# A fused attention and adapter kernel: tokens put into natural order at the x copy, other groups, coarser squares

## The chip, the cores and the metric

The kernel runs on one core of one Trainium2 chip. The metric is the device time of one execution in microseconds (us), taken as the median of several runs.

## The reference

Squared-ReLU attention for 8 batches, 12 heads, 448 tokens and head size 64 gives x; a mixture of eight rank-16 adapters, two chosen per token, is added to it.

```python
# q, k, v: (8, 12, 448, 64) float32
scores = scale * np.matmul(q, k.transpose(0, 1, 3, 2))
attn = np.maximum(scores, 0.0) ** 2 / S
x = np.matmul(attn, v)            # then to (3584, 768): token by (head, dim)
logits = x @ w_gate               # (3584, 8)
topk = the two largest logits of each token
w = softmax over these two
delta = sum over the two experts e of w * ((x @ A[e]) @ B[e])   # A[e]: 768x16, B[e]: 16x768
return x + delta                  # (3584, 768) float32
```

## The kernel before

**Loads.** q, k and v come in by DMAs that POOL issues (line 185), converted to bf16. A partition p of 64 takes seven neighbouring tokens, so token p*7+j lies at partition p in block j. Twelve heads are handled as three "quads" q of four heads. For each batch and quad, PE transposes q and k (L310), and DVE copies the transposed tiles to `qT` (L324, L332).

**Attention.** The scores are made in steps n: one step is one block j of 64 keys against all 448 queries of a batch and quad. `qk` (L449) writes scores into two PSUM banks, `relu` (L468 on ACT, L470 on DVE) brings them as bf16 into a tile `a`, `sq` (L485, DVE) squares a whole tile `a` of two or three steps, and `pv` (L516) multiplies with v and accumulates over j. Batch 7 is cut into a part of 320 columns, done block by block, and one of 128, done four blocks at a time (`PARTS`). Columns of qT stand in the order (j, p), so the result and x do too: permuted tokens.

**x.** When the last j is done, `xt_copy` (L544) brings the two PSUM banks of the result into `xt`, the transposed x in bf16 for all 3584 tokens, with one copy of 448 columns for each bank, on ACT or DVE.

**Adapters.** Tokens are taken in 28 tiles of 128. For a group of up to three tiles, `gate` makes x times (A, w_gate) (`z`, L560), the two largest logits (L581), weights by a sigmoid (L585 to L600), weighted z (`zp`, L604), its transpose (`zt`, L622) and the copy `zT` (L639). For each tile and half (384 columns), `b` (L714) multiplies zT with B in float32. Without more, three identity matrix products (L705) add x in PSUM ahead of it, and a copy (L743, ACT or DVE) brings the sum to `osb`. For tiles in a "turned" group, SP issues six DMA transposes (L655) that bring x from `xt` to `xb`; then the identity products fall away and DVE adds xb while it copies (L734). Before the change these are tiles 15 to 23, three at a time.

**Stores.** As tokens are permuted, `st` (L760) writes a tile in two transfers of 64 rows, each row 7 rows from the next in the output. SP issues nearly all; ACT issues those of tiles 24 and 26 and its half of tile 27.

**Order.** The kernel's program order is written out in the string `ORDER`: each word is an operation with the engine (`:A`, `:D`) and the PSUM bank (`@4`). Every engine goes through its own instructions in that order; waits between engines follow from data and buffers. `POOLS` gives the number of buffers of each kind (11 of `a`, 4 of `osb`, 3 of `xb`). `GROUP` is the largest width of `a`.

Of the kernel before, what the change touches and what calls it, by code (L numbers as in the profile page):

```python
# [10 lines left out]
BF16 = mybir.dt.bfloat16  # L11
# [3 lines left out]
J = 7  # L15
CUT = 3
SPIN = 8
PH = 64
QUADS = 3
NB = 8  # L20
# [9 lines left out]
PARTS = {b: ((0, S, 1),) for b in range(NB)}  # L30
PARTS.update({7: ((0, 320, 1), (320, 448, 4))})


C = dict(late=6, xi=(), om=(), merge_x=0, sqs=(2, 2, 3), xback=(15, 23), xblat=1.4, xbdur=1.35, bx=8, xlag=6, xh=2, apart=3, apcap=1, gl=(3, 1), tqlat=2.0)
GROUP = 2688
POOLS = dict(qT=5, a=11, zp=2, zT=3, osb=4, w=3, q=5, k=5, v=8, xb=3)
# [3 lines left out]
f4 f3 f1 f0 f2 f6 f5 f8 f7 f11 f9 f10 f84@0 f12 f88 f85@2 f90 f89 f13 f87@4 qk0@6 f91 qk1@0 qk2@2 relu0:D qk3@4  # L40
f14 relu1:A relu2:D relu3:A tp2@6 f17 qk4@0 relu4:A te2 qk5@4 qk6@2 sq2 relu5:A tp3@6 f16 f86@0 relu6:A te3 sq0
qk7@0 f15 qk8@4 qk9@6 relu7:A tp4@2 relu8:D relu9:A f18 qk10@0 te4 qk11@4 relu10:A qk12@6 sq4 tp5@2 relu11:A f19
qk13@0 relu12:A te5 tp6@4 f26 relu13:A sq9 qk14@2 qk15@6 tp7 relu14:A f23 sq7 pv0@0 pv1 pv2 relu15:A pv3 qk16@2
te6 pv4 pv5 relu16:A f20 pv6 qk17@6 x13:D pv7@4 relu17:A qk18@2 sq11 pv8 f22 pv9 x12:A qk19@6 relu18:A pv10
qk20@0 relu19:D f21 pv11 relu20:A pv12 pv13 qk21@2 x27:A sq16 qk22@6 f27 qk23@0 relu21:A aw1@5 sq14 relu22:A f33
relu23:A x26:D qk24@2 tp8@6 ae1 f25 relu24:A qk25@0 sq18 qk26@4 tp9 relu25:A f55 pv14@2 pv15 pv16 relu26:A pv17
te8 qk27@0 pv18 f31 pv19 relu27:A pv20 sq23 qk28@4 qk29@6 x41:A f28 qk30@0 relu28:A x40:D aw0@3 sq25 relu29:A
f29 relu30:A qk31@4 tp10@6 ae0 tp11 relu31:A f32 sq21 qk32@0 qk33@2 relu32:A te10 pv21@4 pv22 f30 relu33:A pv23
qk34@0 sq30 qk35@6 relu34:A qk36@2 f37 relu35:D relu36:A qk37@0 pv24 pv25 pv26 relu37:A sq32 qk38@2 f35 tp12@6
pv27 relu38:A tp13 qk39@0 x55:A te12 f43 qk40@2 x54:A z0@5 relu39:A sq35 qk41@6 f34 z1 relu40:A qk42@0 relu41:D  # L50
z2 relu42:A qk43@2 f38 gmax0 relu43:A tp14@6 sq28 qk44@0 tp15 relu44:A f42 qk45@2 gd0 gu0 te14 relu45:A qk46@0
gt0 relu46:A f50 sq39 qk47@6 pv28@2 pv29 pv30 gsg0 pv31 relu47:A qk48@0 f24 pv32 pv33 gw0 sq44 pv34 relu48:A f48
qk49@6 x69:A gzp0 tp18@0 relu49:A tp19 sq37 f36 pv35@4 zt0@3 zt1 zt2 x68:A qk50@6 te18 zT0:A pv36 f41 pv37
relu50:A qk51@2 pv38 sq46 pv39 relu51:A pv40 qk52@0 f47 qk53@6 pv41 relu52:A tp16@2 x82:D tp17 relu53:A te16
qk54@0 b2@4 relu54:A sq49 f44 qk55@6 o2:A qk56@2 qk57@0 relu55:A relu56:D b0@4 f49 x83:A relu57:D qk58@6 o0:A
qk59@2 relu58:A z3@5 z4 f39 sq51 relu59:A qk60@0 qk61@6 z5 sq56 relu60:A b4@4 f40 relu61:A gmax3 qk62@2 sq58
b1@0 relu62:A f46 gu3 gd3 o4:A qk63@6 gt3 sq42 qk64@2 gsg3 o1:A b3@1 f65 relu63:A gw3 b5@4 gzp3 relu64:A sq60
f51 zt3@0 zt4 zt5 o3:A pv42@6 pv43 o5:A qk65@2 st2 pv44 zT3:A pv45 sq53 qk66@4 relu65:A pv46 pv47 pv48 tp20@0
relu66:A st4 qk67@2 tp21 x96:D x97:A f53 te20 pv49@4 relu67:A pv50 qk68@6 st0 pv51 pv52 relu68:A pv53 sq63 f66
pv54 pv55 qk69@0 qk70@2 x110:A relu69:D qk71@6 f45 relu70:A b6@4 relu71:A x111:D qk72@0 o6:D tp22@2 relu72:A  # L60
sq65 qk73@6 tp23 pv56@4 pv57 relu73:A f74 qk74@0 te22 pv58 pv59 relu74:A pv60 qk75@6 f79 pv61 sq67 pv62 relu75:A
qk76@2 b8@0 relu76:A x124:D qk77@6 f64 x125:A sq70 tp24@2 relu77:A tp25 qk78@4 z6@1 te24 f59 relu78:A qk79@6 z7
relu79:A o8:D qk80@4 qk81@2 f52 sq72 z8 relu80:A b10@0 relu81:A gmax6 sq77 f54 qk82@6 tp26@4 o10:A tp27 qk83@2
relu82:A gd6 gu6 b7@0 te26 f56 relu83:A qk84@6 gt6 o7:D qk85@4 gsg6 relu84:A qk86@2 gw6 f70 sq74 b9@0 relu85:A
pv63@6 pv64 relu86:A gzp6 pv65 qk87@4 pv66 sq79 pv67 relu87:A pv68 pv69 zt6@1 zt7 x139:A x138:D zt8 qk88@2 o9:A
qk89@4 zT6:D qk90@6 relu88:A st8 relu89:D tp28@0 tp29 relu90:A qk91@2 f80 te28 pv70@4 pv71 relu91:A pv72 pv73
qk92@6 f60 sq84 pv74 pv75 relu92:A pv76 qk93@0 b14@2 x153:D x152:A f58 relu93:A sq81 qk94@6 tp30@4 o14:A tp31
pv77@0 relu94:A pv78 f77 qk95@2 te30 pv79 pv80 relu95:A pv81 qk96@6 pv82 f57 sq91 pv83 relu96:A qk97@4 b11@2
relu97:D x166:A f67 b12@3 x167:A o11:A sq93 qk98@6 o12:A st10 qk99@0 qk100@4 relu98:A relu99:D b13@2 relu100:A
z9@3 st6 sq88 qk101@6 o13:A tp32@0 qk102@4 relu101:A tp33 b15@2 st12 f62 sq86 relu102:A qk103@6 o15:A te32 f61  # L70
qk104@4 relu103:A z10 z11 sq100 relu104:A qk105@0 f69 pv84@6 pv85 pv86 relu105:A gmax9 qk106@4 pv87 sq95 f72
pv88 relu106:A pv89 pv90 qk107@0 x181:A qk108@4 f63 gd9 gu9 x180:A relu107:D b16@2 relu108:A gt9 qk109@6 o16:D
f81 pv91@0 gsg9 pv92 relu109:A gw9 pv93 sq105 qk110@4 pv94 pv95 relu110:A pv96 f78 qk111@6 gzp9 pv97 relu111:A
x195:D zt9@2 zt10 qk112@4 sq98 x194:A zt11 f75 b17@3 relu112:A zT9:D qk113@6 o17:A sq102 pv98@0 qk114@4
relu113:A pv99 st16 tp36@2 pv100 tp37 relu114:A pv101 qk115@6 te36 pv102 pv103 relu115:A st14 pv104 tp34@4 tp35
f83 sq109 qk116@2 x209:A qk117@6 x208:A b20@1 relu116:A f68 te34 b22@0 relu117:A f71 sq114 o20:A qk118@2 qk119@4
qk120@6 relu118:A b21@1 f73 sq112 o22:A b23@2 relu119:A o21:D z12@3 sq107 relu120:A st20 qk121@0 qk122@4
relu121:A z13 relu122:D z14 o23:A qk123@6 pv105@0 gmax12 pv106 relu123:A qk124@4 gd12 pv107 gu12 pv108 gt12
sq116 pv109 relu124:A pv110 pv111 qk125@6 f82 b18@2 gsg12 relu125:A gw12 x223:D x222:A qk126@4 f76 o18:D qk127@6
relu126:A b19@1 gzp12 sq121 relu127:A zt12@0 zt13 zt14 qk128@2 pv112@4 pv113 o19:D relu128:A qk129@6 pv114  # L80
zT12:D pv115 st18 pv116 relu129:A pv117 sq123 pv118 tp38@2 qk130@0 x236:A tp39 qk131@6 st22 relu130:A b24@4 te38
relu131:A tp42@0 sq119 tp43 x237:A qk132@2 b25@6 relu132:A te42 xb90 b28@7 o24:A o25:A sq128 xb93 qk133@2 o28:A
qk134@4 tp40@0 relu133:A sq126 pv119@6 tp41 pv120 relu134:A pv121 xb91 qk135@2 te40 pv122 pv123 relu135:A pv124
pv125 qk136@4 x251:D xb94 qk137@0 x250:A b29@2 sq130 relu136:A b26@3 st24 relu137:A sq135 o29:A qk138@6 qk139@4
o26:A qk140@0 xb92 z15@2 relu138:A relu139:D z16 z17 relu140:A qk141@6 st28 gmax15 pv126@4 pv127 relu141:A gd15
pv128 gu15 qk142@0 gt15 sq133 pv129 pv130 gsg15 pv131 relu142:A xb108 qk143@6 pv132 gw15 b27@3 gzp15 x264:A
x265:D relu143:A zt15@2 xb111 zt16 zt17 sq137 pv133@0 o27:A qk144@4 tp44@6 zT15:A pv134 tp45 relu144:A xb95
qk145@2 pv135 te44 pv136 relu145:A pv137 qk146@4 pv138 pv139 st26 sq140 relu146:A z18@6 b30@7 x279:A sq142 z19
x278:A xb109 qk147@2 qk148@4 qk149@0 o30 relu147:A z20 sq144 b32@7 relu148:A xb112 relu149:A b33@2 gmax18 xb110
qk150@4 o32 qk151@0 relu150:A b31@3 gu18 o33 relu151:A gd18 qk152@4 sq149 st32 b34@7 relu152:A gt18 o31 gsg18  # L90
qk153@0 qk154@4 gw18 o34 relu153:A b35@2 st30 gzp18 relu154:A qk155@0 o35 pv140@6 relu155:A pv141 sq151 qk156@4
xb113 pv142 pv143 relu156:A qk157@2 qk158@0 pv144 pv145 relu157:D relu158:A pv146 tp46@4 tp47 x293:A x292:D
qk159@0 qk160@2 relu159:A zt18@7 te46 zt19 xb126 zt20 z21@6 relu160:A z22 sq156 zT18:A qk161@0 qk162@4 qk163@2
relu161:A xb129 b40@7 sq147 relu162:A z23 sq158 relu163:A qk164@0 xb127 pv147@4 pv148 pv149 relu164:A pv150
qk165@2 o40 pv151 pv152 relu165:A pv153 sq154 qk166@0 xb130 b41@7 relu166:A gmax21 x307:A gu21 qk167@2 gd21
pv154@0 sq163 x306:A pv155 pv156 st34 relu167:A pv157 pv158 qk168@4 gt21 o41 pv159 gsg21 pv160 b36@2 gw21 x320:A
gzp21 xb128 x321:A b38@3 sq161 relu168:A zt21@7 zt22 sq165 zt23 qk169@0 st40 zT21:A pv161@4 pv162 pv163
relu169:A pv164 qk170@6 o38 pv165 pv166 relu170:A o36 pv167 xb131 b37@3 x335:D x334:A sq168 qk171@0 qk172@6
relu171:A qk173@4 z24@2 o37 z25 relu172:A sq170 st36 b46@3 relu173:A b47@0 o46 b39@1 sq172 b44@3 o47 z26 o39
# [831 lines left out]
```

## Time and profile before

| what | value |
|---|---|
| median of 3 runs | 181.65 us (181.2 to 183.14) |
| the profiled execution's own time | 182.88 us |
| its span, first to last instruction | 180.8 us |
| mean granted TensorE clock | 0.988 |
| PE / DVE / ACT / POOL busy | 165.2 / 163.6 / 156.4 / 89.9 us |
| scores on ACT (L468), 158 | 132.6 us, 952 ns each |
| squares on DVE (L485), 75 | 89.0 us, 1200 ns each |
| B products (L714), 112 | 47.5 us, 515 ns each |
| x copies (L544): ACT 37, DVE 17 | 19.0 us and 9.6 us |
| stores issued by SP, 50 of 192 KB | 3.9 us to landing |
| DMA transposes on SP, 18 | 3.1 us to landing |

Busy time is the time in which at least one instruction of an engine runs; instructions in a row overlap, so busy time is less than count times mean. A share of the span says how full an engine is on the average, not which engine sets the pace in a given stretch. In the views, an engine name followed by q is its queue, and PEld is PE's loading of weights. The span is about 2 us shorter than the execution's time.

### The profile page before, as it was taken

Reading aid. Unit: us, or ns where it says so; the run is one execution under the profiler, and the core shown is the slowest. Engines: PE = TensorE matmul, PEld = TensorE weight load, DVE = VectorE, ACT = ScalarE, POOL = GpSimd, SP = SyncE. Lnnn points to the kernel's source line nnn. Section 1 sums busy time; section 2 is a strip of 40 time slices with the busy share of each in tenths; the row PEclk is TensorE's granted clock in tenths of the full one; section 3 lists DMA queues with packets and bytes.
Section 4 is the critical chain, followed back from the end, with each engine's and each line's share of the span. In section 5 each row is a group of like instructions: output and inputs, shape, how many; then the busy total and the mean of one; then the engine's idle time right before and its main releaser. Section 6 shows DMA issues by size and latency. Waiting matters only on the chain.

```text
span 180.8 us, 7744 instructions
## 1 busy us (share of the span) xinstructions
PE 165.2 (91%) x3366; PEld 99.2 (55%) x3366; DVE 163.6 (90%) x254; ACT 156.4 (87%) x240; POOL 89.9 (50%) x155
## 2 busy tenths in 40 slices
PE   7777889788999999999999899999999999999990
PEld 2434466454555565655646475655666557676640
DVE  0799799999989999999999899999999999999740
ACT  3499899999999999999999999999999899992120
POOL 7998998979669377760877487340000000000000
PEclk9997899999999999999999999999999999999999
DMA  5999999999999999996599999997376579467875
GB/s 94 127 175 180 156 142 179 182 184 164 214 142 146 186 237 194 176 178 141 68 143 287 224 181 259 224 170 202 68 126 144 131 175 110 101 149 176 227 215 172
DMA packets 34450, 30.50 MB, mean 169 GB/s; under 512 B 11952, under 2 KB 30896, under 8 KB 34416
## 3 DMA queue, kind: packets, MB, share of 16 engines
q0 software_dynamic: 22000, 17.03, 64.9%
q1 hardware_dynamic: 11792, 11.90, 26.5%
q10 hardware_dynamic: 624, 1.08, 2.2%
q8 instruction: 26, 0.43, 1.0%
q14 instruction: 8, 0.07, 0.1%
HBM read 33.84 MB, written 11.01 MB: 248 GB/s over the span
## 4 chain that ended last, share of the span: by engine, by line
PE 51%; ACT 27%; POOL 7%; DMA 6%; issue 4%; DVE 3%; ACTq 0%; DVEq 0%; POOLq 0%
ACT a L468 24%; PE ps L714 18%; PE ps L449 11%; PE ps L516 10%; DMA q<-in_q_dram 6%; PE ps L560 4%; PE ps L310 3%; PE ps L705 3%; POOL q L185 3%; POOL k L185 3%; PE ps L622 2%; ACT osb L743 2%; DVE a L485 2%; ACT xt L544 1%; POOL k_rest L216 1%
## 5 line engine op out<-in xcount | busy, mean ns | idle before, releaser
L468 ACT ACTIVATE a<-ps 128x896 bf16<-128x896 f32 (+3 forms) x158 | 132.6, 952 | 3.7 <-PE ps L449 3.1
L485 DVE TENSOR_TENSOR a<-a 128x1792 bf16<-128x1792 bf16 (+3 forms) x75 | 89.0, 1200 | 0.0
L449 PE MATMUL ps<-qT 64*64 64x448 bf16 (+2 forms) x756 | 58.1, 342 | 3.9 <-ACT a L468 2.4
L714 PE MATMUL ps<-B,zT 128*128 128x384 f32 x112 | 47.5, 515 | 0.0
L516 PE MATMUL ps<-a,v 64*64 64x448 bf16 (+2 forms) x756 | 45.3, 335 | 1.6 <-DVE a L485 1.3
L449 PEld LDWEIGHTS <-qT 64*64 64x64 bf16 x756 | 25.1, 105 | 31.8 <-issue 23.2
L185 POOL DMA_DIRECT2D k<-in_k_dram x46 | 27.9, 629 | 18.2 <-PE ps L310 7.3
L185 POOL DMA_DIRECT2D v<-in_v_dram x48 | 29.0, 629 | 6.2 <-PE ps L449 1.8
L185 POOL DMA_DIRECT2D q<-in_q_dram x48 | 29.4, 651 | 4.9 <-DMA v<-in_v_dram 2.7
L516 PEld LDWEIGHTS <-v 64*64 64x64 bf16 x756 | 22.7, 108 | 9.0 <-issue 4.1
L324 DVE COPY qT<-ps 128x1792 bf16<-128x1792 bf16 x21 | 22.8, 1085 | 0.2
L544 ACT CAST xt<-ps 128x448 bf16<-128x448 f32 (+2 forms) x37 | 19.0, 554 | 2.9 <-PE ps L516 2.7
L743 ACT COPY osb<-ps 128x384 f32<-128x384 f32 x26 | 13.1, 523 | 7.1 <-PE ps L714 4.1
L714 PEld LDWEIGHTS ps<-B,zT 128*128 128x128 f32 x112 | 17.3, 190 | 3.3 <-issue 0.3
L470 DVE TENSOR_SCALAR a<-ps 128x896 bf16<-128x896 f32 (+1 forms) x16 | 16.9, 1067 | 0.5 <-PE ps L449 0.5
L310 PEld LDWEIGHTS <-q 64*64 64x64 bf16 x672 | 10.4, 111 | 6.3 <-issue 2.5
L560 PEld LDWEIGHTS <-xt 128*128 128x128 bf16 x168 | 10.5, 98 | 5.8 <-issue 4.7
L560 PE MATMUL ps<-awg,xt 128*128 128x136 bf16 x168 | 13.5, 223 | 0.0
L705 PEld LDWEIGHTS <-xt 128*128 128x128 bf16 x114 | 8.0, 98 | 9.9 <-issue 8.1
L310 PE MATMUL ps<-identb,q 64*64 64x64 bf16 x672 | 10.8, 196 | 2.5 <-DMA q<-in_q_dram 1.3
L705 PE MATMUL ps<-identb,xt 128*128 128x128 bf16 x114 | 12.7, 220 | 0.2
L544 DVE CAST xt<-ps 128x448 bf16<-128x448 f32 (+2 forms) x17 | 9.6, 571 | 2.2 <-PE ps L516 2.2
(47 smaller groups left out, 97.5 us busy)
## 6 DMA issues: line engine op xcount, KB each, us to landing
out_dram<-osb SPq DMA_DIRECT2D x50, 192.0 KB, 3.9
q<-in_q_dram POOLq DMA_DIRECT2D x48, 112.0 KB, 4.8
v<-in_v_dram POOLq DMA_DIRECT2D x48, 112.0 KB, 5.0
k<-in_k_dram POOLq DMA_DIRECT2D x46, 112.0 KB, 5.1
out_dram<-osb ACTq DMA_DIRECT2D x4, 192.0 KB, 2.9
B<-in_moe_B_dram POOLq DMA_DIRECT2D x1, 384.0 KB, 8.0
xb<-xt SPq DMA_TRANSPOSE x18, 3.1
a_raw<-in_moe_A_dram POOLq DMA_DIRECT2D x1, 192.0 KB, 5.2
```

The costliest lines, as they stand in the source:

```text
L185: nc.gpsimd.dma_start(out=t[g * PH : g * PH + PH], in_=k.qkv[w][b, g, :, 2 * q : 2 * q + 2, :])
L310: nc.tensor.transpose(k.ps_b[sl * PH : sl * PH + PH, o.banks[g], (w * J + j) * PH : (w * J + j) * PH + PH], source(w, j)[r, sl], k.identb[ ...
L324: nc.vector.tensor_copy(t.rearrange("p g w x -> p g (w x)"), k.ps_b[:, m.banks[0] : m.banks[0] + 2, : 2 * S])
L449: nc.tensor.matmul(out=bank(o, sl)[g * PH : g * PH + PH, at : at + w], lhsT=t[r, g, 1, j * PH : j * PH + PH], rhs=t[r, g, 0, x0:x1], start ...
L468: nc.scalar.activation(out, flat(qk_ops[n], w), ACTF.Relu, scale=k.relu_scale)
L470: nc.vector.tensor_scalar(out, flat(qk_ops[n], w), k.relu_scale, 0.0, op0=ALU.mult, op1=ALU.max)
L485: nc.vector.tensor_mul(a, a, a)
L516: nc.tensor.matmul(out=bank(head, g)[sl * PH : sl * PH + PH, :w], lhsT=vn[r, sl, j * PH : j * PH + PH], rhs=T["a", g0][r, x + sl * width(n ...
L544: evac(w, lambda cp, g=g: cp(k.xt[:, g * QUADS + q, b * S + x0 : b * S + x1], bank(src, g)[:, :w]), deps=[pv_ops[n]], free=[(src, g)], key ...
L560: nc.tensor.matmul(out=bank(zops[0])[:, t * ZW : t * ZW + ZW], lhsT=k.xt[:, do, 128 * tiles[t] : 128 * tiles[t] + 128], rhs=k.awg[:, do, : ...
L705: nc.tensor.matmul(out=out(h)[:, x * 128 : x * 128 + 128], lhsT=k.xt[:, 3 * h + x, c0 : c0 + 128], rhs=k.identb, start=(x == 0), stop=Fals ...
L714: nc.tensor.matmul(out=o, lhsT=T["zT", g0][:, zi], rhs=rhs, start=xb is not None, stop=True, skip_group_check=True,)
```

## The change

x is brought into natural token order while it is copied from PSUM: the copy reads its source with a step of 64 words and writes without gaps. For batches 0 to 5 one copy takes both banks. Gate groups are cut so that they end with batches (3, 3, 3, 3, 2, 3, 2, 2, 3, 3, 1 tiles). Turned are tiles 17 to 20 in one group of four, 21 to 23 and 24 to 26; 15 and 16 no longer. Stores are single transfers of 128 neighbouring rows. Squares take four and three steps in turn between step 14 and step 140; `a` has 8 larger buffers for 11. Batch 7's parts are 322 and 126 tokens. The string `ORDER` is another one throughout; it is left out here.

```diff
-PARTS.update({7: ((0, 320, 1), (320, 448, 4))})
-C = dict(late=6, xi=(), om=(), merge_x=0, sqs=(2, 2, 3), xback=(15, 23), xblat=1.4, xbdur=1.35, bx=8, xlag=6, xh=2, apart=3, apcap=1, gl=(3, 1), tqlat=2.0)
-GROUP = 2688
-POOLS = dict(qT=5, a=11, zp=2, zT=3, osb=4, w=3, q=5, k=5, v=8, xb=3)
+PARTS.update({7: ((0, 322, 1, (0, 1, 2)), (322, 448, 4, (0, 1, 2)))})
+C = dict(late=6, xi=(), om=(), merge_x=126, sqp=((14, (2, 2, 3)), (140, (4, 3)), (999, (2, 2, 3))), om2=(), fl=(), gf=(3, 3, 3, 3, 2, 3, 2, 2, 3, 3, 1), ai=4, tg=((17, 4), (21, 3), (24, 3)), sp=(), xbdur=1.45, bx=8, xh=2, apart=3, apcap=1, gl=(3, 1), tqlat=2.0)
+GROUP = 3584
+POOLS = dict(qT=5, a=8, zp=2, zT=3, osb=4, w=3, q=5, k=5, v=8, xb=2)
...
 # qk
-                            out=bank(o, sl)[g * PH : g * PH + PH, at : at + w],
-                            lhsT=t[r, g, 1, j * PH : j * PH + PH], rhs=t[r, g, 0, x0:x1],
+                            out=bank(o, sl)[g * PH : g * PH + PH, at : at + w].rearrange("k (j p) -> k j p", j=J),
+                            lhsT=t[r, g, 1, j * PH : j * PH + PH],
+                            rhs=t[r, g, 0].rearrange("d (j p) -> d j p", j=J)[:, :, x0 // J : x1 // J],
...
 # xt_copy
-                evac(2 * w, lambda cp: cp(k.xt[:, q::QUADS, b * S + x0 : b * S + x1], pair(src)[:, :, :w]),
+                evac(2 * w, lambda cp: cp(k.xt[:, q::QUADS, b * S + x0 : b * S + x1].rearrange("d g (p j) -> d g p j", j=J),
+                                       pair(src)[:, :, :w].rearrange("d g (j p) -> d g p j", j=J)),
...
-            evac(w, lambda cp, g=g: cp(k.xt[:, g * QUADS + q, b * S + x0 : b * S + x1], bank(src, g)[:, :w]),
+            evac(w, lambda cp, g=g: cp(k.xt[:, g * QUADS + q, b * S + x0 : b * S + x1].rearrange("d (p j) -> d p j", j=J),
+                                       bank(src, g)[:, :w].rearrange("d (j p) -> d p j", j=J)),
...
 # st
-            r = 0
-            while r < 128:
-                b, x = divmod(c0 + r, S)
-                j, p = divmod(x, PH)
-                m = min(PH - p, 128 - r)
-                if b >= c["bx"]:
-                    j = TURNED[j]
-                {"SP": nc.sync, "ACT": nc.scalar, "POOL": nc.gpsimd}[e].dma_start(
-                    out=k.out[b, j, p : p + m, c1:c2], in_=T["osb", tl][r : r + m, c1:c2])
-                r += m
+            {"SP": nc.sync, "ACT": nc.scalar}[e].dma_start(out=k.out[c0 : c0 + 128, c1:c2], in_=T["osb", tl][:, c1:c2])
...
-    h.out = out.rearrange("(b p j) f -> b j p f", b=NB, j=J)
+    h.out = out
```

## The prediction

> **What bounds the kernel now.** I read the page's busy times first, then busy time by stretch of the span, then the chain of the last stretch, then single instructions.
>
> ```profile
> PE 165.2 (91%) x3366; PEld 99.2 (55%) x3366; DVE 163.6 (90%) x254; ACT 156.4 (87%) x240; POOL 89.9 (50%) x155
> ```
>
> No engine stands out on the average, so the stretches decide. Columns: stretch, its length, busy time of PE, PEld, DVE, ACT, POOL, granted clock, DMA share, GB/s.
>
> ```profile
> 6.00:30.00 24.00, 19.55 (x488) 11.52 (x489) 21.92 (x25) 21.38 (x28) 22.99 (x39) 0.93 1.18 162
> 30.00:60.00 30.00, 26.85 (x607) 15.94 (x603) 29.36 (x42) 30.00 (x46) 24.96 (x43) 1.00 1.13 173
> 60.00:90.00 30.00, 29.40 (x701) 17.93 (x700) 29.90 (x41) 30.00 (x44) 16.64 (x29) 1.00 0.98 169
> 120.00:150.00 30.00, 29.90 (x643) 18.52 (x640) 29.35 (x48) 28.80 (x48) 0.00 (x0) 1.00 0.66 144
> 165.00:171.00 6.00, 6.00 (x105) 4.12 (x95) 5.16 (x22) 1.56 (x7) 0.00 (x0) 1.00 0.79 212
> 171.00:181.00 10.00, 4.89 (x28) 2.65 (x26) 2.79 (x5) 1.13 (x3) 0.00 (x0) 0.95 0.67 191
> ```
>
> Three regimes. Up to 30 us POOL's loads are the bound: POOL 22.99 of 24, PE only 19.55. From 30 to 150 us ACT and DVE are both full and PE nearly so: less work helps there only if it comes off ACT or DVE. From about 161 us (the last score product ends at 160.88) PE alone is the bound. The chain of the last stretch says it exactly (start, length, what):
>
> ```profile
> 173.28 0.17 PE ps L705 x3
> 173.45 0.70 PE ps L714 x2
> 174.15 0.17 PE ps L705 x3
> 174.32 0.70 PE ps L714 x2
> 175.02 0.17 PE ps L705 x3
> 175.19 0.71 PE ps L714 x2
> 175.90 0.02 issue
> 175.92 0.56 DVE osb L743
> ```
>
> Each output half of tiles 24 to 27 costs 0.17 us for three identity products that add x and 0.70 us for z times B. After the last copy come stores; the timeline has ACT's queue issuing them from 174.70 for 2.94 us, so to 177.64, and the span ends 3.2 us later at 180.8.
>
> **What consecutive instructions really cost.** Mean durations overlap their neighbours, so I take distances between starts in the timeline (start, length, what):
>
> ```profile
> 69.41 1.08 DVE L324 COPY qT<-ps 128x1792 bf16<-128x1792 bf16 x1
> 70.41 1.55 DVE L485 TENSOR_TENSOR a<-a 128x2688 bf16<-128x2688 bf16 x1
> 71.88 0.62 DVE L544 CAST xt<-ps 128x448 bf16<-128x448 f32 x1
> 72.41 1.08 DVE L485 TENSOR_TENSOR a<-a 128x1792 bf16<-128x1792 bf16 x1
> 73.41 1.08 DVE L324 COPY qT<-ps 128x1792 bf16<-128x1792 bf16 x1
> ```
>
> A square of 1792 takes 1.00 us, of 2688 1.47 us: 0.47 us per 896, hence 0.06 us fixed and 1.94 us for 3584 (estimate from these two). An x copy of 448 takes 0.53 on DVE. On ACT seven scores in a row take 5.89 us, 0.82 each, and a 448 copy 0.42 (start 64.10, next start 64.52).
>
> **The change, part by part**, with instruction counts from the two orders of instructions.
>
> *Coarser squares.* 75 squares become 57 over the same elements: 18 x 0.06 = -1.1 us of DVE.
>
> *x copied whole.* 24 copies of 448 on ACT become 12 of 2x448, on DVE 12 become 6: 12 x (2 x 0.42 - 0.82) = -0.2 us on ACT, 6 x (2 x 0.53 - 1.00) = -0.4 on DVE. This uses the contiguous price for reads that now step 64 words through PSUM at every element; see the second rival. By the Trainium skill ("ScalarE: Activation LUTs", What ACT_TABLE_LOAD costs) an instruction with immediates has 186 ns fixed, of which 93 ns overlap, so 12 merged pairs would save 12 x 93 ns, about 1.1 us; the starts above show 0.02 us each, so I do not take it.
>
> *Other moves between ACT and DVE.* Outputs: ACT copies 26 to 22, at 0.365 us (two in 0.73), -1.5; DVE adds 18 to 20 and copies 12 to 14, +1.9 at 0.47. zT: DVE -0.9, ACT +0.8. One more gate group (11 for 10): DVE +0.6, ACT +0.2. The remaining score and x shapes come to +0.3 on ACT, -0.2 on DVE. Summed: ACT -0.4, DVE -0.1. So in the full stretch the change is worth almost nothing: I take -0.2.
>
> *Tiles 15 and 16 by PE, 24 to 26 by transposes.* After the last score product the order now has 14 output halves in place of 15 (-0.70) and 2 identity triples in place of 8 (6 x 0.17 = -1.02): -1.72 us on the engine that sets the end. Cover: the six transposes of tiles 24-26 come on SP's queue between stores, about 1.25 us each and 3.1 us to landing; the last two wait for the last large x copies, but the first add needing them stands behind the whole gate of tiles 24-26 and several B products, over 5 us of PE work. Without that cover it would be up to +2. DVE makes all their adds, at 0.5 us against PE's 0.70 per half, and still keeps up. Before the last score product PE gets one half and four triples more, +1.4 us; PE has 4.7 us idle between 30 and 165 us, mostly early, so I take +0.4 (0 to +1.4).
>
> *Plain stores.* One issue of 128 rows for two of 64. Between tiles nothing waits for SP. At the end ACT and SP each issue one transfer for two: an issue takes 1.18/2 = 0.59 us, so -0.59 (bounds -0.6 to +0.3, if one larger transfer lands later by half a landing spread). The stores of tiles 4 and 9 now stand far back in SP's order and each holds one of the four output buffers for long; the next users of the remaining buffers come 7 or more scores (over 5 us) after the store before them, above the 3.9 us of a landing. Cost 0, up to +1.
>
> *Start.* v of the first triple is loaded two loads earlier (about 2.4 us), so value products can fill PE's holes (4.45 us idle from 6 to 30 us); but the two selector operations (0.84 and 0.83 us) move ahead of the next batch's k on POOL. PE's waits for loads are short:
>
> ```profile
> PE ps L310 <- DMA q<-in_q_dram: 1.3, 3, 0.6
> PE ps L516 <- DVE a L485: 1.3, 2, 0.7
> ```
>
> I take -0.5 (-1.5 to +1.5).
>
> *Sum.* -0.2 - 1.72 + 0.4 - 0.59 - 0.5 = -2.6 us. The profiled execution took 182.88 us (span 180.8 and 2.1 around it), so 180.3 there. It lay 1.23 us above the median of the runs, 181.65; against the median the forecast is 179.0 us. With the bounds the case spans 176.5 to 180.5.
>
> **Rivals.**
>
> *1. The tail gain is given back.* PE is full from 120 us on (29.90 of 30), so the +1.4 us moved ahead of the last score product may count whole, and the denser end (1.40 us per tile for 1.74, with 393 KB each, so 280 GB/s where the last stretches show 191 to 212) may wait for output buffers, about +0.7. Then -2.6 + 1.0 + 0.7 = -0.9: 180.8 us. Against: 0.67 DMA share at 191 GB/s leaves room to about 285.
>
> *2. The stepped PSUM read is slow: slower than before.* Every x copy now writes natural order, reading words 256 bytes apart. No row of this trace steps so. The nearest rows that show one engine at two rates by form are DVE's: 1792 bf16 in 1.00 us against 896 f32 from PSUM in 1.00, a factor of two, which I use as the upper bound; the lower is no penalty. ACT reads 14,850 such elements per partition (12 x 896, 4 x 448, 6 x 322, 3 x 126) at 0.91 ns: doubled +13.5 us, some 12 of it in the full stretch, where nothing hides it because the engine of each instruction is fixed. DVE would get +7.4 beside it. Time 191 at a factor of two, 182 at a quarter more; it decides from about a fifth more per copy (2.6 of 12). Centre 187. I take no penalty because these copies handle one f32 word per step, already the slow form. The Trainium skill speaks against me ("Advanced Engine Details and Errata", PSUM Cachelines): PSUM lines hold two f32 values, and accesses should come in contiguous pairs for best throughput, said of matmuls. No run here shows it yet.
>
> *3. Coarse squares block DVE.* A square of 3584 holds DVE 1.94 us; a score or transposed-q copy behind it waits, and PE behind that. The waits row shows up to 0.7 us for one. At 0.3 us for 18 squares, +5.4, less the gain: 184.5. For: DVE has no idle time. Against: value products stand seven scores behind the scores that they need, which covers one square.
>
> **How the numbers follow.** Forecast 0.58, rival 1 0.15, rival 2 0.17, rival 3 0.10. A measurement of this kernel tells about 1% from no change: faster is below 179.8, slower above 183.5. Forecast gives 0.52 faster, 0.06 same; rival 1 0.02, 0.10 and 0.03 slower; rival 2 0.02 same, 0.15 slower; rival 3 0.10 slower. Sums: 0.54, 0.18, 0.28. The range 176.0 to 186.0 leaves out the strong half of rival 2 and a gain beyond every bound; the forecast's own range is 176.5 to 180.5.
>
> **What would show it.** Right: ACT's 2x448 copies at about 0.99 us mean like the 896 scores; the last score product near 160 us; 13.3 us of PE from there to the last product, with 0.70 us steps for tiles 24 to 26; one store issue per queue after the last copy. Wrong: 2x448 copies above 1.2 us (rival 2); PE waiting for DVE's squares by several us (rival 3); the last product as late as 175 us, or output copies waiting for stores (rival 1).

## The result, and the profile after

The changed kernel takes 187.16 us (median of 5 runs), the one before 182.57 us (5 runs): a ratio of 1.0258, 95% interval 1.0211 to 1.0306. The change costs 2.6%. The forecast was 179.0 us. The ratios here and below are not quotients of the medians: they leave out executions more than 1.5% above the fastest of their kernel, which are two of these five, two of e1's four, five of twelve in e10 and in e15, and up to three of twelve elsewhere. The profiled execution took 189.69 us, of which some 2.8 us go with a low clock at its end, as will be seen; it is read for waits and order, and totals come from the ratios.

In each of the following views the line numbers are those of the kernel shown: L451 is `qk`, L471 `relu`, L488 `sq`, L519 `pv`, L559 the whole x copy, L643 `zt`, L676 the transpose, L727 the identity product, L736 `b`, L763 the add of a turned tile, L772 the plain output copy, L782 the store.

The page, busy times. No engine has become much fuller; what grew is the span, by 7 us to 187.9.

```profile
PE 168.2 (90%) x3360; PEld 100.5 (54%) x3360; DVE 163.4 (87%) x238; ACT 155.6 (83%) x227; POOL 90.3 (48%) x155
```

Busy time by stretch (stretch, its length, PE, PEld, DVE, ACT, POOL, granted clock, DMA share, GB/s):

```profile
120.00:150.00 30.00, 30.00 (x605) 18.83 (x598) 29.12 (x47) 28.95 (x48) 1.19 (x2) 1.00 0.50 119
...
165.00:171.00 6.00, 6.00 (x121) 4.46 (x120) 5.15 (x17) 2.04 (x6) 0.00 (x0) 1.00 0.26 52
171.00:181.00 10.00, 6.04 (x17) 2.92 (x15) 4.86 (x15) 0.21 (x1) 0.00 (x0) 0.75 0.81 294
181.00:188.00 7.00, 2.63 (x8) 1.22 (x7) 0.93 (x2) 0.48 (x1) 0.00 (x0) 0.74 0.31 115
```

Up to 171 us PE is as full as before. From 171 us PE has holes and a clock of 0.75. Just before, from 165 to 171 us, the DMAs move only 52 GB/s at a share of 0.26: whatever comes late there does not wait for bandwidth.

The page's groups name waits of the output operations (line, engine, operation, tiles, count | busy, mean ns | idle before, and what ended it). No output operation waited for a store before.

```profile
L772 ACT COPY osb<-ps 128x384 f32<-128x384 f32 x22 | 11.0, 505 | 9.4 <-DMA out_dram<-osb 9.1
...
L763 DVE TENSOR_TENSOR osb<-ps,xb 128x384 f32<-128x384 f32 x20 | 10.5, 551 | 6.0 <-DMA out_dram<-osb 3.9
```

The chain of the last stretch (start, length, what) shows where those stores had been:

```profile
163.30 1.01 ACT a L471
164.31 0.65 ACT xt L564 x2
...
166.10 1.21 SPq L676
...
167.36 2.68 SPq L676
...
170.10 2.57 DMA out_dram<-osb
...
172.69 1.02 DVE osb L763 x2
...
174.12 2.52 DMA out_dram<-osb
...
176.73 0.56 DVE osb L763
...
177.74 0.48 PE ps L643
178.22 2.57 PE ps L736 x4
```

Two stores end waits in this chain, and the first could not be issued before 170.10 because SP was busy with transposes (SPq L676). SP's queue in order of time says why:

```profile
153.81 2.71 SPq L782 DMA_DIRECT2D out_dram<-osb  x3
162.44 7.60 SPq L676 DMA_TRANSPOSE xb<-xt  x4
170.10 1.05 SPq L782 DMA_DIRECT2D out_dram<-osb  x2
171.24 2.78 SPq L676 DMA_TRANSPOSE xb<-xt  x2
```

SP does nothing from 156.5 to 162.4 us. Its own waits name what it waits for, in the stretch from 150 us (who, for whom: us, times, longest):

```profile
SPq L676 <- DVE osb L763: 5.9, 1, 5.9
```

The next instruction in SP's queue is the first transpose of tiles 24 to 26, and it waits for a DVE add. The transposes write `xb`. The change has three turned groups and cuts `POOLS` from `xb=3` to `xb=2`, so the third group takes the buffer of the first (tiles 17 to 20), and that is free only when the last add of tile 19 has read it. DVE makes these last adds here:

```profile
160.89 1.49 DVE L763 TENSOR_TENSOR osb<-ps,xb 128x384 f32<-128x384 f32 x3
...
172.69 1.02 DVE L763 TENSOR_TENSOR osb<-ps,xb 128x384 f32<-128x384 f32 x2 [2.44 <-DMA out_dram<-osb]
...
176.73 0.56 DVE L763 TENSOR_TENSOR osb<-ps,xb 128x384 f32<-128x384 f32 x1 [1.51 <-DMA out_dram<-osb]
```

The first three end at 162.38, and SP goes on at 162.44. Behind its four transposes (7.60 us) stand the stores of tiles 18 and 19, whose data were complete by 162.4 and which go out at 170.10. Until then they hold two of the four output buffers; the adds of tile 21 and then of tile 25 wait for one (2.44 and 1.51 us), and with them PE:

```profile
PE ps L736 <- DVE osb L763: 2.4, 1, 2.4
```

At the end the clock adds to the damage. PE is mostly idle from 172 to 178 us, and then four B products take 2.57 us, 0.64 each. The first line is PE's longest pause, in brackets; the others are stretches as above, with the granted clock third from the end:

```profile
175.27 0.91 PE L736 MATMUL ps<-B,zT 128*128 128x384 f32 x2 [2.40 <-DVE osb L763]
...
176.00:178.00 2.00, 0.44 (x2) 0.26 (x2) 1.24 (x4) 0.00 (x0) 0.00 (x0) 0.52 1.02 402
178.00:180.00 2.00, 2.00 (x5) 1.09 (x5) 1.28 (x4) 0.00 (x0) 0.00 (x0) 0.50 0.53 209
180.00:182.00 2.00, 2.00 (x7) 1.00 (x6) 0.65 (x2) 0.00 (x0) 0.00 (x0) 0.50 0.52 203
```

In the profile of e2, below, the same products take 0.32 us. The Trainium skill ("TensorE: Matmul & The Clock Gate", Part 1: The HAM clock gate) says that PE falls to half clock after an idle window of some 3.4 us. The granted 0.50 agrees with the half. The length is not what these runs show: PE worked 2.05 us in the 6 us from 172 to 178, and its longest pause before the clock fell was 2.40 us. In e1, below, a pause of 2.26 us was followed by 0.50 as well; in e15 one of 1.42 us left the clock at 1.00.

### The profile page after: what moved, and what is told of

Read it like the earlier page. It is cut to its first block, busy times and chain, and to the rows that moved or that the text cites. A ratio compares the mean times of both kernels' runs of the same rounds, so it can differ in the third digit from the quotient of the medians.

```text
span 187.9 us, 7650 instructions
## 1 busy us (share of the span) xinstructions
PE 168.2 (90%) x3360; PEld 100.5 (54%) x3360; DVE 163.4 (87%) x238; ACT 155.6 (83%) x227; POOL 90.3 (48%) x155
## 4 chain that ended last, share of the span: by engine, by line
PE 42%; ACT 24%; DMA 12%; DVE 7%; issue 5%; POOL 5%; SPq 2%; ACTq 0%; DVEq 0%; POOLq 0%
ACT a L471 20%; PE ps L736 11%; PE ps L451 11%; PE ps L519 9%; DMA k<-in_k_dram 5%; DMA out_dram<-osb 4%; PE ps L312 4%; DMA q<-in_q_dram 3%; PE ps L581 3%; PE ps L727 2%; POOL q L184 2%; SPq L676 2%; ACT xt L559 2%; DVE a L488 2%; PE ps L643 1%
## 5 line engine op out<-in xcount | busy, mean ns | idle before, releaser
L471 ACT ACTIVATE a<-ps 128x896 bf16<-128x896 f32 (+2 forms) x158 | 131.9, 942 | 6.5 <-PE ps L451 5.7
L488 DVE TENSOR_TENSOR a<-a 128x2688 bf16<-128x2688 bf16 (+5 forms) x57 | 85.9, 1524 | 0.0
L451 PE MATMUL ps<-qT 64*64 64x448 bf16 (+2 forms) x756 | 60.0, 346 | 4.7 <-ACT a L471 2.0
L736 PE MATMUL ps<-B,zT 128*128 128x384 f32 x112 | 48.9, 533 | 2.4 <-DVE osb L763 2.4
L519 PE MATMUL ps<-a,v 64*64 64x448 bf16 (+2 forms) x756 | 45.0, 334 | 0.2 <-ACT a L471 0.2
L451 PEld LDWEIGHTS <-qT 64*64 64x64 bf16 x756 | 24.9, 106 | 33.5 <-issue 26.5
L519 PEld LDWEIGHTS <-v 64*64 64x64 bf16 x756 | 23.1, 107 | 8.8 <-issue 2.5
L736 PEld LDWEIGHTS ps<-B,zT 128*128 128x128 f32 x112 | 18.6, 201 | 6.7 <-DVE osb L763 3.3
L772 ACT COPY osb<-ps 128x384 f32<-128x384 f32 x22 | 11.0, 505 | 9.4 <-DMA out_dram<-osb 9.1
L473 DVE TENSOR_SCALAR a<-ps 128x896 bf16<-128x896 f32 (+2 forms) x16 | 16.9, 1060 | 1.5 <-PE ps L451 1.0
L763 DVE TENSOR_TENSOR osb<-ps,xb 128x384 f32<-128x384 f32 x20 | 10.5, 551 | 6.0 <-DMA out_dram<-osb 3.9
L581 PE MATMUL ps<-awg,xt 128*128 128x136 bf16 x168 | 13.3, 223 | 0.4 <-ACT xt L559 0.4
L727 PE MATMUL ps<-identb,xt 128*128 128x128 bf16 x108 | 12.5, 226 | 0.7 <-ACT xt L559 0.4
L312 PE MATMUL ps<-identb,k 64*64 64x64 bf16 x644 | 10.6, 196 | 1.8 <-DMA k<-in_k_dram 1.8
L727 PEld LDWEIGHTS <-xt 128*128 128x128 bf16 x108 | 7.5, 101 | 8.5 <-issue 7.8
L312 PE MATMUL ps<-identb,q 64*64 64x64 bf16 x672 | 10.3, 195 | 1.7 <-DMA q<-in_q_dram 1.5
```

Source lines behind the costliest of these rows:

```text
L312: nc.tensor.transpose(k.ps_b[sl * PH : sl * PH + PH, o.banks[g], (w * J + j) * PH : (w * J + j) * PH + PH], source(w, j)[r, sl], k.identb[ ...
L451: nc.tensor.matmul(out=bank(o, sl)[g * PH : g * PH + PH, at : at + w].rearrange("k (j p) -> k j p", j=J), lhsT=t[r, g, 1, j * PH : j * PH ...
L471: nc.scalar.activation(out, flat(qk_ops[n], w), ACTF.Relu, scale=k.relu_scale)
L473: nc.vector.tensor_scalar(out, flat(qk_ops[n], w), k.relu_scale, 0.0, op0=ALU.mult, op1=ALU.max)
L488: nc.vector.tensor_mul(a, a, a)
L519: nc.tensor.matmul(out=bank(head, g)[sl * PH : sl * PH + PH, :w], lhsT=vn[r, sl, j * PH : j * PH + PH], rhs=T["a", g0][r, x + sl * width(n ...
```

## The experiments

The theory (the queue theory, Q in the expectations): the whole loss is this one wait of SP, a shortage of `xb` buffers that holds transposes, behind them stores, behind them output buffers. Against it stood that the transposes are late by themselves, that the loss lies in the attention phase (theory M; more PE work there, the coarse squares, or the stepped or whole x copies), and that three turned groups are simply too many. Ratios are against the kernel before, run on the same chip beside it, with their 95% interval; single executions of one kernel lie up to 4% apart, so 1 us needs the ratios. Line numbers shift by a few from kernel to kernel. "Last scores" is the end of the last `qk` in a kernel's profile: 160.88 us before, 163.23 after, with the last product at 175.90 and 183.6.

**e1: the four transposes behind the two stores.** A change of `ORDER` alone.

```diff
-... xb144 ... xb147 ... xb145 ... xb148 ... st36 ... st38 x334:A ...
+... st36 ... st38 xb144 xb147 xb145 xb148 x334:A ...
```

> The changed kernel, only with the first four transposes of tiles 24-26 placed behind the stores of tiles 18 and 19 on SP. Theory Q (SP's queue: the transposes wait for the transpose buffer and the x copies while finished tiles stand behind them unsent, so output buffers run out at the end): these two stores go out near 163 us of the span and not at 170, the adds' wait of 2.4 us goes, and the time falls by 2 to 4 us, to about 184. Theory M (the loss lies in the attention phase, more work on TensorE and later loads, and the end only shows it): same time within 1 us.

Measured: 1.0154 [1.0057, 1.0252], from two executions. By its middle less than half of the loss is gone; with both intervals, a gain is not certain. The profile shows the order: SP's queue now sends the two stores (L780) in time, and the transposes (L674) are what comes late; the chain's wait has changed its name:

```profile
152.66 8.92 SPq L780 DMA_DIRECT2D out_dram<-osb  x5
161.67 9.34 SPq L674 DMA_TRANSPOSE xb<-xt  x6
171.11 8.75 SPq L780 DMA_DIRECT2D out_dram<-osb  x5
```

```profile
167.18 3.63 DMA xb<-xt
...
171.11 2.52 DMA out_dram<-osb
```

With two `xb` buffers, whichever of the two goes first on one queue, the other is late. The half clock comes again, after a pause of 2.26 us:

```profile
174.73 0.35 PE L641 MATMUL ps<-identf,zp 128*128 128x128 f32 x1 [2.26 <-DVE zp L623]
...
176.00:178.00 2.00, 2.00 (x7) 1.06 (x6) 0.89 (x2) 0.00 (x0) 0.00 (x0) 0.50 0.99 387
```

**e2: a third xb buffer.**

```diff
-..., v=8, xb=2)
+..., v=8, xb=3)
```

> The changed kernel with three transpose buffers for two, so that the transposes of tiles 24-26 need not wait until the adds of tiles 17-20 have freed one. Theory Q: they leave SP some 3 us sooner, the stores of tiles 18 and 19 too, time down 1.5 to 3 us. Theory M: no change.

Measured: 182.06 us, 0.9989 [0.9924, 1.0055]: the loss is gone, with order, groups, squares and copies of the changed kernel untouched. SP's queue:

```profile
156.12 5.21 SPq L676 DMA_TRANSPOSE xb<-xt  x4
161.43 2.60 SPq L782 DMA_DIRECT2D out_dram<-osb  x2
164.12 2.52 SPq L676 DMA_TRANSPOSE xb<-xt  x2
166.72 8.94 SPq L782 DMA_DIRECT2D out_dram<-osb  x5
```

The four transposes begin 6.3 us earlier (156.12 for 162.44) and the two stores 8.7 us earlier. No add or copy waits for a store any more, and the chain ends as a chain of PE:

```profile
172.55 1.29 PE ps L736 x4
173.84 0.17 PE ps L727 x3
174.01 0.70 PE ps L736 x2
174.71 0.17 PE ps L727 x3
174.88 0.71 PE ps L736 x2
175.59 0.02 issue
175.61 0.48 ACT osb L772
```

The two profiles can be set against each other from the last scores on. From 162.44 to the `zt` of the last tile (172.44) e2 needs 10.0 us, the changed kernel 14.5 (163.23 to 177.74): 4.5 us more, of which PE's two pauses are 2.40 and 1.56. From there to the last copy e2 needs 3.2, the changed kernel 5.9: 2.8 us of half clock.

**e15: six output buffers instead, xb left at two.**

```diff
-..., osb=4, w=3, ..., xb=2)
+..., osb=6, w=3, ..., xb=2)
```

> The changed kernel as it is (two transpose buffers) with six output buffers for four. Theory Q has two parts: late transposes and, behind them, stores that hold the output buffers. With two more buffers no add or copy waits for a store; the waits for the transposes themselves stay. So the time falls by 2 to 3.5 us from 187, to 184 or 185, and not to e2's 182. If the waits for output buffers are the whole loss: 182; if only the transposes' lateness counts: no change.

Measured: 1.0148 [1.0110, 1.0185], so 1.1 of the 2.6% are gone. SP's idle time is still there, 5.9 us long, and the transposes run from 160.20 only; no add waits for a store, but one waits 1.9 us for its transpose:

```profile
DVE osb L763 <- DMA xb<-xt: 1.9, 1, 1.9
...
PE ps L736 <- DVE osb L763: 1.4, 1, 1.4
```

On one base of 181.7 us the stages are: changed 186.4, stores first 184.5, six output buffers 184.4, three xb buffers 181.5. Each is uncertain by 0.7 to 1.8 us. Of 4.9 us, 2.0 (uncertain by 1.1) are output buffers held by stores that stand behind transposes, and 2.9 (uncertain by 1.4) are left where no add waits for a store. In e15's profile the late transposes make the way from the last scores to the last product 15.00 us (161.29 to 176.29) for e2's 13.15, at a clock of 1.00; what makes the rest of the 2.9 was not shown.

**e3: tiles 24 to 26 not turned.** Their adds go back to identity products, as before the change.

```diff
-tg=((17, 4), (21, 3), (24, 3))     ORDER: xb144 to xb149; o48 to o53 as DVE adds
+tg=((17, 4), (21, 3))              ORDER: none of these;  o48:D o49:A o50:A o51:D o52:D o53:A
```

> The changed kernel with tiles 24-26 not transposed by DMA: identity products add x again (18 more, 1.0 us of TensorE after the last scores), and their output copies are shared between ACT and DVE. Theory Q: SP only stores at the end, no add or copy waits for a store, and in spite of the 1.0 us the time falls by 3 to 4.5 us, to 183 or 184. Theory M: it rises by 1 us.

Measured: 1.0100 [1.0030, 1.0170], between e2 and the changed kernel. Without a third group two buffers are enough and no stall is there, but PE has its six triples back: last scores at 162.91, last product at 177.35, so 14.4 us against 13.15 in e2. The third group, given a buffer of its own, is worth 1.3 us by the two profiles and 2.0 by the two ratios, whose intervals are some 1.2 us to either side.

**e6: the coarse squares cut in two.** On top of e2, each square of 3584 as two instructions of 1792.

```diff
-            nc.vector.tensor_mul(a, a, a)
+            h = 1792 if total == 3584 else total
+            for y in range(0, total, h):
+                nc.vector.tensor_mul(a[:, y : y + h], a[:, y : y + h], a[:, y : y + h])
```

> The changed kernel with three transpose buffers (e2), every square of 3584 made by two instructions of 1792 in the same place. If the coarse square saves what two starts in a row say, 18 x 0.06 us, DVE has 1.1 us more to do and the last scores end up to 1 us later than in e2; if coarse squares block what stands behind them, earlier by 1 us or more. No change beyond 0.5 us: their size does not matter.

Measured: 1.0035 [1.0001, 1.0069], against 0.9989 for e2, with last scores at 162.48 against 162.44. There is no sign that coarse squares block anything, and 18 instructions fewer bring no time that could be told.

**e10: PE work taken out of the middle.** e2 without the identity products of tiles 11 to 16, 12 triples or 2.04 us of PE.

```diff
-                for x in range(0 if xb or xi else 3):
+                for x in range(0 if xb or xi or 11 <= tl <= 16 else 3):
...
-                    start=xb is not None, stop=True, skip_group_check=True,
+                    start=xb is not None or 11 <= tl <= 16, stop=True, skip_group_check=True,
```

> The changed kernel with three transpose buffers (e2), with the identity products of tiles 11 to 16 left out, so that their outputs lack x: 12 triples of 0.17 us, 2.0 us of TensorE, between about 110 and 150 us. If TensorE sets the pace there: last scores 2.0 us earlier than in e2 and time 2.0 us less, near 180. If ACT and DVE set it: no more than 0.5 us earlier; then the products moved ahead of the last scores are not what makes the changed order's last scores late.

Measured: 0.9939 [0.9899, 0.9980], last scores at 161.70. For 2.04 us less PE work that is 0.74 us at the last scores and 0.9 by the ratios. But the changed kernel, e2 and e15, with all of that work in the same order, have theirs at 163.23, 162.44 and 161.29, further apart than 0.74 although only numbers of buffers differ. Whether PE sets the pace before the last scores, as its 30.00 of 30 us from 120 to 150 suggests, stays open.

**e4: natural order and plain stores alone.** The new code with the order, groups, turned tiles, squares and x copies of before.

```diff
-merge_x=126, sqp=((14, (2, 2, 3)), (140, (4, 3)), ...), gf=(3, 3, 3, 3, 2, ...), tg=((17, 4), (21, 3), (24, 3)); GROUP = 3584; a=8, xb=2
+merge_x=0, sqp=((999, (2, 2, 3)),), gf=(), tg=((15, 3), (18, 3), (21, 3)); GROUP = 2688; a=11, xb=3; ORDER of before
```

> The kernel before with only the natural order of tokens: stepped x copies of one bank each, one store of 128 rows per tile, parts of 322 and 126; order, groups, turned tiles 15-23 and squares as before. Theory Q and theory M alike: the stepped copies cost nothing, the end has one store issue less per queue, so 0.5 to 1 us faster than the kernel before, 181 to 182. A theory that the natural order itself costs (stepped reads, larger stores landing later): 185 or more.

Measured: 1.0015 [0.9937, 1.0093], no change. From the last copy to the end of the span it takes 3.9 us, for 4.3 before and 4.3 in e2. Over all the profiles here this stretch is 2.9 to 4.9 us long, so what one store for two saves at the end cannot be told.

**e8: e4 with tiles 15 to 17 not turned.**

```diff
-tg=((15, 3), (18, 3), (21, 3))     ORDER: xb90 to xb95; o30 to o35 as DVE adds
+tg=((18, 3), (21, 3))              ORDER: none of these; o30:D to o35:D as copies
```

> The natural order alone (e4), and tiles 15-17 not turned: 18 identity products more on TensorE before the last scores (6 triples of 0.17 us, 1.0 us), output copies on DVE as before, six transposes less on SP. If TensorE sets the pace from 120 us on: last scores 1.0 us later than in e4 and the time 1.0 us longer. If TensorE's idle time covers it: no change.

Measured: 0.9995 [0.9958, 1.0032]. Six triples more, 1.02 us of PE, are not to be seen; but the difference from e4 is uncertain by 1.6 us, so that they are free there is not shown.

**e5, e12, e14: the third turned group in the old order.** e5 is e4 with tiles 24 to 26 turned and a buffer of their own (`xb=4`); e12 turns 24 and 25 only; e14 is e5 with six output buffers.

```diff
-tg=((15, 3), (18, 3), (21, 3)), xb=3, osb=4
+e5:  tg=(..., (24, 3)), xb=4;  ORDER: xb144 xb147 after xb131, xb145 xb148 after x334, xb146 after st36, xb149 after st46, o48 to o53 on DVE
+e12: as e5, but tg=(..., (24, 2)), o52:A o53:A
+e14: as e5, with osb=6
```

> The natural order alone (e4), and tiles 24-26 turned besides 15-23, with four transpose buffers; their six transposes stand where their x copies are long done, none ahead of a finished tile's store by more than two. Theory Q says that turning the last tiles pays once SP isn't blocked: six identity triples less after the last scores, 6 x 0.17 us, so 1.0 us faster than e4: last product about 14 us after the last scores instead of 15, about 180.5 us. Rival: SP's stores come late again and the end is as long as in e4 or longer.

> e5 with tiles 24 and 25 turned, not 26, whose output copies go to ACT: two triples more on TensorE at the end (0.34 us), two adds less on DVE (1.0 us). In e5 the end ran through DVE: TensorE waited 0.5 us for the last gate behind the adds. If that wait is worth more than the triples: 0.2 to 0.5 us faster than e5; if TensorE alone sets the end: 0.3 us slower.

> e5 (order of before, natural tokens, tiles 24-26 turned too) with six output buffers for four. If output buffers held by stores that leave late still cost at the end of e5, up to 0.7 us faster than e5, about 180.3 us; if not, the same.

Measured: e5 0.9966 [0.9931, 1.0000], e12 0.9950 [0.9919, 0.9980], e14 0.9939 [0.9908, 0.9970], with a median of 180.78 us the lowest found: about 0.6% under the kernel before. The three do not stand apart by their intervals, and e4's overlaps them. The profiles tell more: from the last scores to the last product e4 needs 15.03 us, e5 14.50, e14 14.33 and e12 15.08. In e12's profile a store wait of the familiar kind is still in the chain:

```profile
166.24 3.80 DMA out_dram<-osb
```

and in those of e5 and e14 none is, though their chains run through DVE's adds there. So turning the last tiles shortens the end in the old order by 0.5 to 0.7 us, half to two thirds of the 1.02 us of the six triples; the 0.9 us between the ratios of e4 and e5 are uncertain by 1.6.

**e7, e9, e11, e13: the form of the x copies.** e7 and e9 are e4 with whole x copies, every third on DVE; e7 puts each at the place of the later of the two halves, e9 at that of the earlier. In e7 the next product then overwrites one bank before it is copied, so a part of its x is not the reference's, and e9 replaces it. e11 is e5 with the copies of e9. e13 goes the other way: e2 with each whole copy cut in two halves side by side, one on ACT and one on DVE.

```diff
-e4:  ... x27:A ... x26:D ...   merge_x=0
+e7:  ... x26:A ...             merge_x=126   (in the place of x26:D)
+e9, e11: ... x26:A ...         merge_x=126   (in the place of x27:A)
-e2:  ... x12:A ...             merge_x=126
+e13: ... x12:A x13:D ...       merge_x=0
```

> The natural order alone (e4), and the two banks of x of batches 0 to 5 copied by one instruction, in the place of the later of the two. By starts in a row 0.2 us of ACT and 0.4 us of DVE less: same time as e4 within 0.5 us, a copy of 2x448 at 0.95 us on ACT and 1.09 on DVE. Rival: the two banks come free later and the next value products wait, 1 us slower or more.

> The natural order alone (e4), and the two banks of x of batches 0 to 5 copied by one instruction in the place of the earlier of the two, where both banks are finished. By starts in a row 0.2 us of ACT and 0.4 us of DVE less: e4's time within 0.5 us. Rival: a copy of 2x448 holds its engine for twice as long and scores behind it come late, 1 us slower or more.

> The order of before with natural tokens, tiles 24-26 turned too (e5), and x copied whole as in e9. If whole copies save what starts in a row say, 0 to 0.5 us faster than e5: about 180.6 us, 0.5 per cent under the kernel before.

> The changed kernel with three transpose buffers (e2), x of batches 0 to 5 again copied by two instructions, one on ACT and one on DVE in the same place, 448 columns each. In the order of before whole copies cost 5 us and more (e9); if they cost here too, the last scores end 2 us or more earlier than in e2 and the time falls to 180 or less. If this order was laid out around whole copies: same as e2 within 0.7 us, or slower, as each engine is interrupted twice as often.

Measured: e7 1.0475 [1.0430, 1.0521], e9 1.0317 [1.0281, 1.0354], e11 1.0261 [1.0217, 1.0305], e13 1.0436 [1.0381, 1.0490]. All four lose 5 to 9 us. If whole copies were dear, e13 was to gain, and it lost. The copies themselves (L556) cost in e9 what they cost elsewhere:

```profile
L556 ACT CAST xt<-ps 128x896 bf16<-128x896 f32 x12 | 11.3, 944 | 0.5 <-PE ps L516 0.5
```

What is lost is lost between engines. From 30 to 150 us PE, DVE and ACT of e4 are busy for 115.25, 117.88 and 118.40 of 120 us; those of e9 for 110.74, 112.03 and 113.15, 4.5 to 5.9 us less. In e13 they are at 110.21, 110.97 and 111.60, and its waits show the scores on PE (L449) behind copies of qT and x on DVE (L324, L562):

```profile
PE ps L449 <- DVE qT L324: 3.0, 5, 1.3
...
PE ps L449 <- DVE xt L562: 2.3, 4, 1.0
```

e13 also puts 12 more x copies on DVE, 18 halves for 6 whole ones, and that is a part of its loss; its size was not separated. What follows is narrower than hoped: an order written by hand fits the lengths that it was written for, and a change of form inside it cost more here than the form. So the middle parts of this change (order, groups, copies) cannot be priced one by one in this way.

## Why the prediction was wrong, point by point

**The step that failed is the cover of the transposes of tiles 24 to 26**, "come on SP's queue between stores", with "between tiles nothing waits for SP" beside it. It asked when their data are there and who needs them, and not where they are written. The diff has `xb=2`, the change has three turned groups, and each group but the first two must wait for an older one's last reader: SP stood 5.9 us before the first of them. The bound "up to +2" without cover, for which the prediction gives no working, was too small. The cure by one buffer is worth 4.9 us (e2): 2.0 of it, uncertain by 1.1, through stores that stand behind the transposes (e15), which the prediction had at "cost 0, up to +1" and for another reason, the early stores of tiles 4 and 9. And an idle PE then fell to half clock, which cost 2.8 us in the profiled execution and was in no step. The transposes took 1.9 us each here (7.60 for four) and 1.3 in e2 (5.21), where 1.25 had been used.

**The range did not follow from the bounds.** The terms' own bounds, without the +2 for a lost cover, add up to -4.0 and +2.3 us on 181.65, so 177.6 to 183.9, where 176.5 to 180.5 was given. The 187.16 lies outside both.

**Rival 1** had the mark right, output copies that wait for stores, and the cause wrong: it spoke of 280 GB/s, and the wait arose at 52. Its 0.7 us for it came from bandwidth.

**The tail's PE work was right.** From the last scores to the last product 13.3 us were forecast; e2, without the stall, has 162.44 to 175.59, 13.15.

**What was to come before it was not.** The last scores were to come some 0.3 us earlier than the 160.88 before (-0.2, +0.4 and -0.5); in e2 they come 1.56 us later, and in the other profiles of the changed order with its whole copies at 161.29 (e15) to 163.23 (the changed kernel). The -0.5 for the start was not found. How much of the lateness is the extra PE work of +1.4, of which +0.4 was taken, is open after e10. There is no sign that it is the squares (e6), and e13 shows only that the order belongs to its copies. The granted clock is low early on (0.58 from 12 to 18 us in e2, 0.85 before), but e15, with 0.50 there, has the earliest last scores of this order, so that was not shown to be the cause. That is how e2, with 1.9 us gained at the end, comes out even with the kernel before: -0.2 us, where the forecast for the change was -2.6. With the missing buffer restored the forecast would have been missed too.

**The store's -0.59 was not found.** The issue did become shorter, but from the last copy to the end of the span it takes 4.3 us before and in e2, and 2.9 to 4.9 over the other profiles.

**Rivals 2 and 3 fell.** A stepped PSUM read takes no longer than a contiguous one here (L559 steps, L471 and L473 do not):

```profile
L471 ACT ACTIVATE a<-ps 128x896 bf16<-128x896 f32 x133 | 114.2, 976 | 4.5 <-PE ps L451 4.4
...
L473 DVE TENSOR_SCALAR a<-ps 128x896 bf16<-128x896 f32 x14 | 15.1, 1085 | 1.4 <-PE ps L451 1.0 <-ACT a L471 0.2
...
L559 ACT CAST xt<-ps 128x896 bf16<-128x896 f32 x12 | 11.4, 953 | 0.0
...
L559 DVE CAST xt<-ps 128x896 bf16<-128x896 f32 x6 | 6.5, 1088 | 0.1
```

On ACT the 896 stepped elements take 953 ns, the 896 contiguous ones of a score 976; on DVE it is 1088 and 1085. The forecast of 0.99 us on ACT was about right. The rule on contiguous pairs (the Trainium skill, "Advanced Engine Details and Errata", PSUM Cachelines), said of matmuls, does not carry over to these two readers in this case. For coarse squares that block DVE there is no sign (e6).

## What to carry to other kernels

When a diff adds an instruction to a queue that runs in order, look up the buffer that it writes: count the users of the pool against its size, find the last reader of the one that it replaces, and then list what stands behind it in the queue and which buffers those hold. One small number in a table of pool sizes cost 4.9 us here, more than the 2.6 us that the whole change was to gain, and showed itself as a wait for stores, three steps from its cause. In a static order, a part that is tried alone is tried in an order made for another part; a loss then says little about the part.

## What the runs showed of the hardware

- Reads of PSUM with a step of 64 words (256 bytes) ran at the speed of contiguous ones on ACT and DVE (953 and 1088 ns for 896 elements, contiguous 976 and 1085).
- A store of 128 rows of 3 KB, neighbours in DRAM, holds SP for a median of 372 ns (332 to 572); one of 64 rows that lie seven apart, before, 588 ns. The landing, at twice the size, took 3.0 us in the changed kernel, 3.2 in e2 and 4.3 in e4, for 3.9 before.
- The last six DMA transposes of the changed kernel held SP's queue for 1.20 to 2.68 us each, 1.34 at the median, 3.3 us to landing.
- At the end PE's granted clock fell to 0.50, and a B product took 0.64 us for 0.32, after a pause of PE of 2.40 us (the changed kernel) and of 2.26 us (e1); after one of 1.42 us (e15) it stayed at 1.00, with four products in 1.29 us.
